# Max of three products rewritten as one part plus the relu of differences, with new PSUM pools and a new order, in an attention and feed-forward kernel

## Chip, cores, metric

One core of one Trainium2 chip. The metric is device time in microseconds (us), measured on the chip; the kernel before runs in about 255 us. A program on one core has no second die to compare with; runs over 1.5% above the fastest of their kernel count as slow and are left out of the ratios. The runs were made in jobs on several chips, and in each job the kernel before ran on the same chip in the same rounds; so kernels are compared by their ratio to it.

## The reference, cut to what matters

Batch 8, 8 heads, 576 positions, head size 64, 32 memory slots, model width 512, inner width 768.

```python
a = softmax(phi, over the 576 positions)           # (b, h, s, 32)
k_m, v_m = a^T k, a^T v                            # 32 x 64 a head
attn = softmax(q @ k_m^T / 8, over the 32 slots)
x = attn @ v_m                                     # heads side by side: (b*s, 512)
h = max(max(x @ w1, x @ w2), x @ w3)               # (b*s, 768)
out = h @ w_out                                    # (b*s, 512), float32
```

Both kernels never form x. For each batch they fold v_m into the weights (`wp` = v_m @ w, 256 x 768 for each of the three) and multiply `attn` by the folded weights.

## The kernel before

The parts that the argument touches; `...` marks cuts. P is 128, NG 2 (groups of four heads), FT 6 (768/128), S 576, SH 288, BANK 512. PSUM is where the matmuls put their results; BANK, 512 numbers a partition, is what the kernels take for one bank of it. The schedule is by hand: the order in which the instructions are written is kept.

```python
acc_pool: bufs=2, PSUM      # tiles of two banks: scores, sums, feed-forward accumulators
one_pool: bufs=4, PSUM      # tiles of one bank: transposes, k/v sums, folds, output tiles

def fold(b, ft):                                   # six a batch
    for g in range(NG):
        wps = one_pool.tile([P, 3, P], FP32)
        for i in range(2):                         # block-diagonal v: 128 rows, 64 columns
            matmul(wps[64*i : 64*(i+1)], lhsT=vm[:, 2*g+i], rhs=w_sb[:, 2*g+i, :, ft*P:(ft+1)*P])
        (scalar if g == 0 else vector).copy(out=wp[:, g, ft], in_=wps)

def ffn1(b, ft, w):                                # 6 x 3 = 18 groups a batch
    acc = acc_pool.tile([P, 2, BANK], FP32)
    ...                                            # four matmuls of 288 columns
    if w == 0:   nc.scalar.copy(out=h1, in_=a)
    elif w == 1: nc.vector.tensor_tensor(out=h2, in0=a, in1=h1, op=max)
    else:        nc.vector.tensor_tensor(out=hT[:, ft, ...], in0=a, in1=h2, op=max)

def ffn2(b, t):                                    # four or five output tiles a batch
    ...                                            # six matmuls of 512 columns, ScalarE copies, store
# order: attention(0), fold/ffn1(0), ffn2(0), attention(1) in one piece, folds(1); then for each
# batch its 18 ffn1 groups, with the next batch's attention and folds and the last batch's output
# tiles put between them at fixed fractions of the 18
```

The softmax here doesn't subtract the row's maximum and nothing guards it: scores larger than these inputs give would overflow.

## Time and profile before

| | before |
|---|---|
| median of the first 3 runs | 255.34 us (255.06 to 257.24) |
| span in the profiled run | 253.2 us, mean granted TensorE clock 0.96 |
| PE / VectorE / ScalarE busy | 195.2 / 139.1 / 121.5 us |
| one steady batch | 26.6 us |

PE is the matmul engine, DVE is VectorE, ACT is ScalarE; `L288 PE MATMUL acc<-attn,wp` is the work of line 288, its output tile and its inputs.

### The profile page before, as it was taken

The page shows a single profiled execution, that of the slowest core. Times are in us where ns is not written, and L with a number is a line of the kernel's source. Part 1 is how long each engine was busy: PE and PEld are TensorE (multiplying, and loading weights), DVE is VectorE, ACT ScalarE, POOL GpSimd, SP SyncE. Part 2 cuts the span into 40 slices and gives each one's busy share as a digit, 9 for nine tenths or more (in the row PEclk, how much of TensorE's full clock was granted, in tenths as well). Part 3 has the DMA queues.
Part 4 walks back from the last instruction along what each step waited for, and adds up shares of the span by engine and source line. Part 5 has one row for each costly group of instructions (what it writes and reads, how often), then busy time and mean ns, then how long its engine had stood idle before and what let it go on. Part 6 is the DMA issues. An engine that isn't in the chain of part 4 may idle for free.

```text
span 253.2 us, 3962 instructions
## 1 busy us (share of the span) xinstructions
PE 195.2 (77%) x1589; PEld 111.0 (44%) x1608; DVE 139.1 (55%) x252; ACT 121.5 (48%) x213; POOL 29.9 (12%) x45
## 2 busy tenths in 40 slices
PE   0176878586797889889788998897988998888970
PEld 0152333262473356445554565354734573355430
DVE  7354565056546764685196639473677465764400
ACT  2315333618524763575429462856277625733340
POOL 8533200040040003100220022000000000000000
PEclk9996799978897999999999999999999999999997
DMA  5999999999469205991397639950001500720177
GB/s 134 207 203 203 253 207 254 194 231 206 70 131 207 41 0 124 205 212 41 96 155 126 133 106 174 205 134 3 1 3 40 126 3 0 166 45 0 35 159 180
DMA packets 22786, 31.71 MB, mean 125 GB/s; under 512 B 1008, under 2 KB 17136, under 8 KB 22768
## 3 DMA queue, kind: packets, MB, share of 16 engines
q0 software_dynamic: 17776, 22.02, 47.4%
q1 hardware_dynamic: 4992, 9.44, 16.5%
q8 instruction: 12, 0.20, 0.3%
q14 instruction: 6, 0.05, 0.1%
HBM read 39.32 MB, written 9.44 MB: 193 GB/s over the span
## 4 chain that ended last, share of the span: by engine, by line
PE 47%; DVE 24%; ACT 18%; issue 4%; DMA 3%; POOL 1%; DVEq 0%; POOLq 0%
PE acc L288 19%; PE po L319 14%; DVE h L301 6%; ACT e_bd L128 6%; PE kvp L139 6%; DVE hT L304 6%; PE wps L264 5%; ACT ln L246 4%; DVE qT L189 3%; ACT h L298 3%; DMA kvo<-in_v_dram 3%; ACT r L252 3%; DVE kvn L155 2%; DVE wp L275 2%; DVE kmT L167 1%
## 5 line engine op out<-in xcount | busy, mean ns | idle before, releaser
L288 PE MATMUL acc<-attn,wp 128*128 128x288 bf16 x576 | 93.4, 295 | 17.4 <-ACT ln L246 4.8
L288 PEld LDWEIGHTS <-wp 128*128 128x128 bf16 x576 | 53.4, 99 | 52.9 <-issue 27.1
L301 DVE TENSOR_TENSOR h<-acc,h 128x576 bf16<-128x576 f32 x48 | 36.2, 754 | 50.4 <-PE acc L288 36.3
L319 PE MATMUL po<-wo_sb,hT 128*128 128x512 bf16 x197 | 48.2, 379 | 1.5 <-issue 0.5
L298 ACT CAST h<-acc 128x576 bf16<-128x576 f32 x48 | 30.6, 638 | 36.1 <-PE acc L288 35.7
L304 DVE TENSOR_TENSOR hT<-acc,h 128x576 bf16<-128x576 f32 x48 | 36.3, 756 | 8.3 <-PE acc L288 5.2
L329 ACT COPY ost<-po 128x512 f32<-128x512 f32 x32 | 18.7, 585 | 40.6 <-PE po L319 40.5
L275 DVE CAST wp<-wps 128x384 bf16<-128x384 f32 x48 | 26.2, 551 | 12.3 <-PE wps L264 12.0
L139 PE MATMUL kvp<-kvo,e_bd 128*64 128x192 bf16 x288 | 16.0, 264 | 19.7 <-DMA kvo<-in_v_dram 11.6
L319 PEld LDWEIGHTS <-hT 128*128 128x128 bf16 x216 | 20.7, 98 | 21.0 <-DVE hT L304 1.1
L273 ACT CAST wp<-wps 128x384 bf16<-128x384 f32 x48 | 22.9, 479 | 11.9 <-PE wps L264 11.6
L264 PE MATMUL wps<-w_sb,vm_bd 128*64 128x384 bf16 x192 | 26.0, 352 | 2.6 <-ACT wp L273 1.9
L139 PEld LDWEIGHTS <-e_bd 128*64 128x64 bf16 x288 | 12.9, 118 | 24.4 <-issue 13.3
L224 ACT ACTIVATE e<-sc 128x320 bf16<-128x320 f32 (+1 forms) x32 | 11.2, 414 | 25.8 <-PE sc L214 25.8
L128 ACT ACTIVATE e_bd<-ph 64x1152 bf16<-64x1152 f32 x16 | 18.6, 1161 | 4.0 <-DMA ph<-in_phi_dram 3.9
L253 DVE TENSOR_TENSOR attn<-e,r 128x576 bf16<-128x576 bf16 x16 | 12.1, 754 | 11.4 <-ACT r L252 11.4
L97 POOL DMA_DIRECT2D ph<-in_phi_dram x8 | 6.2, 772 | 94.3 <-ACT e_bd L128 90.6
L264 PEld LDWEIGHTS <-vm_bd 128*64 128x64 bf16 x192 | 7.6, 110 | 15.0 <-issue 13.7
L252 ACT ACTIVATE r<-ln 128x576 f32<-128x576 f32 x16 | 10.9, 682 | 0.5
L189 DVE COPY qT<-pt 128x1024 bf16<-128x1024 bf16 x16 | 10.8, 681 | 0.3 <-PE pt L186 0.2
L214 PE MATMUL sc<-qT,kmT 64*32 64x320 bf16 (+1 forms) x128 | 5.4, 300 | 7.1 <-DVE h L301 5.6
L246 ACT ACTIVATE ln<-sm 128x576 f32<-128x576 f32 x16 | 10.4, 650 | 0.2
(33 smaller groups left out, 91.7 us busy)
## 6 DMA issues: line engine op xcount, KB each, us to landing
out_dram<-ost SPq DMA_DIRECT2D x16, 512.0 KB, 5.3
ph<-in_phi_dram POOLq DMA_DIRECT2D x8, 576.0 KB, 4.6
kvo<-in_k_dram POOLq DMA_DIRECT2D x8, 576.0 KB, 6.4
kvo<-in_v_dram POOLq DMA_DIRECT2D x8, 576.0 KB, 8.9
qq<-in_q_dram POOLq DMA_DIRECT2D x8, 576.0 KB, 9.5
w_sb<-in_moe_w_dram POOLq DMA_DIRECT2D x6, 384.0 KB, 14.7
out_dram<-ot SPq DMA_DIRECT2D x8, 128.0 KB, 2.4
wo_sb<-in_moe_w_out_dram POOLq DMA_DIRECT2D x1, 768.0 KB, 18.6
```

Of the source, the lines that this page charges most:

```text
L128: nc.scalar.activation(out=e_bd[r, :, :, a, :], in_=ph[r], func=AF.Exp)
L139: nc.tensor.matmul(kvp[HP * i : HP * (i + 1), g, :], lhsT=e_bd[:, j, c], rhs=kv[:, :, j, c, :], start=(c == 0), stop=(c == NC - 1), tile_p ...
L246: nc.scalar.activation(out=ln.rearrange("p (h n) -> p h n", h=2), in_=sm[:, :, 0:SH], func=AF.Ln,)
L264: nc.tensor.matmul(wps[HP * i : HP * (i + 1)], lhsT=s["vm"][:, 2 * g + i], rhs=w_sb[:, 2 * g + i, :, ft * P : (ft + 1) * P], start=True, s ...
L273: nc.scalar.copy(out=s["wp"][:, g, ft], in_=wps)
L275: nc.vector.tensor_copy(out=s["wp"][:, g, ft], in_=wps)
L288: nc.tensor.matmul(acc[:, h, 0:SH], lhsT=s["wp"][:, g, ft, w, :], rhs=s["attn"][:, g, h * SH : (h + 1) * SH], start=(g == 0), stop=(g == N ...
L298: nc.scalar.copy(out=s["h1"], in_=a)
L301: nc.vector.tensor_tensor(out=h2, in0=a, in1=s["h1"], op=ALU.max)
L304: nc.vector.tensor_tensor(out=hT[:, ft, (b % 2) * S : (b % 2 + 1) * S].rearrange("p (h n) -> p h n", h=2), in0=a, in1=s["h2"], op=ALU.max,)
L319: nc.tensor.matmul(po, lhsT=hT[:, fc, c0 : c0 + P], rhs=wo_sb[:, fc, :], start=(fc == 0), stop=(fc == FT - 1),)
L329: nc.scalar.copy(out=osts[b][:, t], in_=po)
```

## The change

Its intent: max(a,b,c) = c + max(relu(a-c), b-c). The differences w1-w3 and w2-w3 are made once on the chip; c @ w_out goes through `w3o` = w3 @ w_out, also made once, folded per batch and added by two more matmuls in each output tile. So 12 accumulator groups a batch remain of 18, with one VectorE max in each pair. The folds use 64x32 tiles of the TensorE array, eight at a time, in two-bank tiles. PSUM is divided anew, the order of instructions is written out step by step, w3 and w_out load ahead of w1 and w2, and a batch's output is stored in smaller pieces (256 KB instead of 512).

```diff
-    acc_pool bufs=2;  one_pool bufs=4
+    acc_pool bufs=3;  one_pool bufs=2
-    load(0); w1,w2,w3 first halves; w1,w2,w3 second halves; w_out; load(1)
+    load(0) in two parts; w3; w_out; w1,w2 first halves; w1,w2 second halves; load(1)
+    def w3_t(f2): ...    # 24 transposes of w3
+    def w3_o(j): ...     # 24 matmuls of 512 columns: w3o = w3 @ w_out
+    def w_diff(i, h):    # four, VectorE, 16 bits, 1536 elements a partition
+        tensor_tensor(w_sb[:, :, i, half[h]] -= w_sb[:, :, 2, half[h]])
+    def slot(g, a): return a ^ (g & 1)
     def fold(b, n):                                # four a batch: three for w1-w3, w2-w3, one for w3o
+        ps = acc_pool.tile([P, NG, BANK], FP32)
+        for g, i, a: sl = slot(g, a); h4 = 2*i + sl
+            matmul(ps[32*h4 : 32*(h4+1), g, :], lhsT=vm[64 rows of a, 32 columns],
+                   rhs=w_sb[64 rows of a, ...] or w3o[...], tile_position=(64*a, 32*h4))
+        (scalar if n % 2 == 0 else vector).copy(out=..., in_=ps)      # 1024 columns
     def ffn1(b, n):                                # 12 groups a batch
-        w == 0: scalar copy; w == 1: vector max; w == 2: vector max
+        w == 0: scalar relu; w == 1: vector max
     def ffn2(b, t):
+        for g in range(NG): matmul(po, lhsT=attn[:, g, ...], rhs=wp3[b][:, g, :])
     ...
-    fill lists of positions for each batch
+    order = "F0 B0 B1 N T0 F1 Q0 F2 Q1 Q2 F3 K T1 F4 S0 S1 L F5 D0 F6 M0 T2 "
+            "D1 F7 X0 M1 D2 F8 X1 T3 F9 D3 E0 F10 T4 E1 F11"
```

In the order F is a first-product group, T an output tile, E the exp of phi, B and N the k/v sums and their scaling, Q and K transposes, S scores, M softmax sums with Ln and Exp, X their product, D a fold, L a load. Attention of batch 1 is now mixed with the output tiles of batch 0.

## The prediction

> **What bounds the kernel now.** I read the page's busy shares first, then the chain that ended last, then the costliest groups, then the busy time of each engine in stretches of one batch, and last the timeline of one batch. Busy shares, chain and groups, from the page of the kernel before:
>
> ```profile
> PE 195.2 (77%) x1589; PEld 111.0 (44%) x1608; DVE 139.1 (55%) x252; ACT 121.5 (48%) x213; POOL 29.9 (12%) x45
> ...
> PE 47%; DVE 24%; ACT 18%; issue 4%; DMA 3%; POOL 1%; DVEq 0%; POOLq 0%
> ...
> L288 PE MATMUL acc<-attn,wp 128*128 128x288 bf16 x576 | 93.4, 295 | 17.4 <-ACT ln L246 4.8
> L301 DVE TENSOR_TENSOR h<-acc,h 128x576 bf16<-128x576 f32 x48 | 36.2, 754 | 50.4 <-PE acc L288 36.3
> L319 PE MATMUL po<-wo_sb,hT 128*128 128x512 bf16 x197 | 48.2, 379 | 1.5 <-issue 0.5
> L298 ACT CAST h<-acc 128x576 bf16<-128x576 f32 x48 | 30.6, 638 | 36.1 <-PE acc L288 35.7
> L304 DVE TENSOR_TENSOR hT<-acc,h 128x576 bf16<-128x576 f32 x48 | 36.3, 756 | 8.3 <-PE acc L288 5.2
> L275 DVE CAST wp<-wps 128x384 bf16<-128x384 f32 x48 | 26.2, 551 | 12.3 <-PE wps L264 12.0
> L273 ACT CAST wp<-wps 128x384 bf16<-128x384 f32 x48 | 22.9, 479 | 11.9 <-PE wps L264 11.6
> ```
>
> PE is busy 77%, but holds only 47% of the chain; VectorE and ScalarE hold 42% between them. So the chain hops PE, ScalarE, VectorE. The first feed-forward product (L288) has three accumulators per 128 columns: one is copied by ScalarE, two go through a VectorE max. Only two accumulators exist, so PE often waits for an evacuation. Two neighbouring batches, from the stretches view (PE, weight loads, DVE, ACT, POOL busy), and the same stretches for the second product's tile `po` alone (PE, ACT):
>
> ```profile
> 93.10:119.60 26.50, 23.84 (x204) 13.64 (x206) 16.33 (x30) 15.14 (x29) 2.98 (x4) 1.00 0.71 139
> 119.60:146.30 26.70, 22.40 (x195) 13.07 (x197) 16.52 (x30) 14.85 (x28) 2.97 (x4) 1.00 0.65 126
> ```
> ```profile
> 93.10:119.60 26.50, 6.65 (x27) 2.93 (x5) 1.00 0.71 139
> 119.60:146.30 26.70, 5.40 (x22) 2.34 (x4) 1.00 0.65 126
> ```
>
> One batch takes 26.6 us. The first stretch does a fifth output tile that the second does not, 1.25 us of PE, and is not longer. So PE has slack, some 3 to 4 us a batch; the accumulator hand-over is what repeats. DMA runs at 0.65 to 0.71 of its engines and has slack there.
>
> **What the Trainium skill says.** (1) "TensorE: Matmul & The Clock Gate", section "Back-to-back issue gap": N/2.4 + 2.5 ns for a warm matmul. That is 216 ns for 512 columns; the trace agrees (six `po` matmuls hold the chain for 1.29 us, 215 ns each). For 288 columns it is 122 ns, 0.49 us for a group of four; the trace shows 1.15 us for two groups together and 0.65 for a lone one. I use 0.53 to 0.56. (2) "TensorEngine Tiling (Array Packing)", "Key Properties": different tiles execute in parallel, and changing the mode drains the engine. Trace: eight 64x32 score matmuls begin at 131.86 and the next work at 132.11, so 0.25 us for eight, where one after another they would take 0.97 by the formula above. The same page's "Gotcha 1" says that different row tiles cannot access one PSUM bank at once. The scores put each row half in its own bank; the new fold writes both row halves into one bank, in other columns of the array, so no row of this trace settles it. (3) "VectorE: DVE Perf Modes", "The perf-mode tier table": `tensor_tensor` with any PSUM operand runs at 1x; its formula (N+151)/0.96 gives 757 ns for 576, and the trace has 754 to 756. For the new 16-bit SBUF subtraction it allows 2x: estimate (768+151)/0.96 = 0.96 us for 1536 elements.
>
> **The change, part by part, for one steady batch.**
>
> Identity: max(a,b,c) = c + max(relu(a-c), b-c). The c part goes through w3@w_out, so 12 accumulators remain of 18.
>
> First product: 48 matmuls of 72, six groups of four fewer at 0.56 us: PE -3.4 us. Six VectorE maxes go: -6 x 0.755 = -4.5 us. ScalarE's six copies become six relus of the same size: 0.
>
> Second product: two more 512-column matmuls for each tile, 4.5 tiles a batch on the mean: 4.5 x 2 x 0.215 = +1.9 us of PE.
>
> Fold: before, 24 matmuls in six bursts, each holding PE 0.44 to 0.5 us with its drain, 2.8 us. After, four bursts of eight 512-column matmuls. If all eight overlap, a burst is about 0.22 + 0.2 of drain, estimated from the score burst: 1.7 us; if the two row halves take turns, 0.65 us: 2.6. I take 2.0: -0.8 us. Evacuations: from 638 ns for 576 and 479 for 384, ScalarE pays 0.83 ns an element plus 160, so 1.01 us for 1024; VectorE from 551 for 384 at 1.04 ns an element gives 1.22. ScalarE 2 x 1.01 instead of 6 x 0.479: -0.9 us. VectorE 2 x 1.22 instead of 6 x 0.551: -0.9 us.
>
> Exp of phi in four pieces instead of two: 2.73 instead of 2.32 us, ScalarE +0.4. The transposed k and v: VectorE 0.84 instead of 1.0.
>
> Sums. PE by its holding times: first product 6.7, second 7.75, k/v sums 1.8, transposes 1.55, scores 0.6, sums 0.55, folds 2.0: 21.0 us, where the same count for before gives 10.1 + 5.8 + 2.8 + 4.5 = 23.2 of 26.6. VectorE falls from 16.4 to about 11.2, ScalarE from 15.0 to 14.5. With three accumulators of two banks instead of two, and one max in the hand-over instead of two in a row, most of the 3.4 us of waits should go. What stays: the new order puts some 11 us of ScalarE work (two fold copies, two Ln/Exp pairs, exp of phi, relus, `ost` copies) behind the first fold, beside 9 to 10.7 us of PE. I allow 1 us for that: **22 us a batch**, PE-bound.
>
> **Start.** In before, the last first-product group of batch 0 is done and `po` begins at 42.1; batch 1's first product begins at 63.3, after a serial attention. In after, fold 0 needs w1 and w2 less w3. The weights and wo are, together with batch 0, the same bytes in another order; the last weight transfer of before (wo, issued 11.72, 18.6 us to landing) landed at 30.3, so I expect the last piece of w1/w2 there. Subtraction, three folds: 32. ScalarE then does batch 1's exp (2.7 us, phi landing about 33) ahead of the first relu: 36. Twelve groups at 0.53: 42.5, no gain. The w3 transposes and w3@w_out (24 matmuls each, some 7 us) hide under the load. Then attention 1 is interleaved with four output tiles: 4 x 1.72 + 1.8 + 1.55 + 0.6 + 0.55 + 2.0 = 13.4 and some 2.6 of waits: batch 1's first product begins at **58.5**, 5 us earlier.
>
> **Sum.** 58.5; batch 1, which has no output tiles beside it, 18; five batches at 22 = 110; batch 7 with 12 groups (6.4) and four tiles (6.9) and 1.2 of waits = 14.5; five last tiles of eight matmuls 8.8; from the last PE work to the end, 7.8 in before (245.4 to 253.2), a little less with smaller stores: 7.4. Total span 217.2; the measured median was 2.1 above the span: **219.3, say 219 us**, 14% less.
>
> **Rivals.** A: the gain is PE's sum alone, since waits stay as long as before (3.4 us a batch): 24.4 a batch, 5 x 2.4 + 3 more: about 234. For it: the waits may be semaphore and in-order queue delays, not accumulator shortage, and the one-bank pool shrinks from four to two while it serves `po`, transposes and k/v sums. Against it: the missing 1.25 us above shows that PE work fills waits, so they are not fixed delays.
> B: ScalarE becomes the bound. Its sum of 14.5 is far below 22, but in the second half of a batch it has about 11; with no slack there a batch is 23.5: about 228.
> C: the start gets worse: everything needs all weights, and w3@w_out adds a stage. If folds start only at 36 and PE runs at a lower clock after idling (granted clock 0.59 in 20 to 25 us of before), the start is 63 and the time 224.
> D: everything packs well, eight-fold overlap and no waits: 20.5 a batch and a start at 56: about 208.
> Slower than before would need over 27 us a batch; nothing in the sums is near it.
>
> **Range and chances.** C and B with half of A make 230; D makes 209. Range 210 to 231 around 219. Faster by over 2% means under 250: 0.96; within 2%: 0.03; slower: 0.01.
>
> **What would show it.** A steady batch of 21 to 23 us with PE busy above 90% of it, and PE's share of the chain above 65%. VectorE's total near 100 us, ScalarE's near 120. Relus of 638 ns, maxes of 756, fold copies near 1.0 (ACT) and 1.2 (DVE), subtractions near 1 us. A fold burst of 0.4 us if the eight overlap, 0.65 if the bank forces turns. First product of batch 0 ending near 42, of batch 1 beginning near 58. I am wrong if waits for the two one-bank buffers (transposes behind `ost` copies) appear on PE, if the first folds wait for weights beyond 33, or if ScalarE's queue holds accumulators.

## More of the kernel before

In the lists of waits, "A <- B: x, n, m" says that A sat idle x us in n places, at most m, until B was done. The PE rows that matter for the buffers, from the list of waits of the kernel before:

```profile
PE sc L214 <- DVE h L301: 5.6, 6, 1.9
PE acc L288 <- ACT ln L246: 4.8, 6, 0.8
PE acc L288 <- ACT h L298: 3.4, 14, 0.3
```

In each, PE wants to write a new accumulator and waits until an evacuation of an earlier one, of other data, has ended: the two-bank buffers are what it lacks.

## The result

216.91 us, median of 4 runs (216.11 to 218.64), against 255.68 (4 runs) for the kernel before. The ratio is 0.8485 (95% interval 0.8418 to 0.8552). Ratios here are the mean time of one kernel's fast runs over that of the other's of the same rounds, so not quite the ratio of the medians. The predicted 219 was 1% high.

Busy shares, the chain that ended last and costly groups, from the page of the changed kernel (in a group: its count, busy us and mean ns of one, then the idle us of the engine just before and what ended most of it):

```profile
PE 175.2 (82%) x1589; PEld 101.7 (47%) x1608; DVE 103.1 (48%) x168; ACT 119.8 (56%) x201; POOL 32.0 (15%) x48
...
PE 59%; ACT 16%; DVE 12%; issue 5%; DMA 5%; POOL 2%; DVEq 0%; ACTq 0%; POOLq 0%
...
L365 PE MATMUL acc<-attn,wp 128*128 128x288 bf16 x384 | 60.1, 286 | 7.5 <-ACT h L375 5.2
L377 DVE TENSOR_TENSOR hT<-acc,h 128x576 bf16<-128x576 f32 x48 | 36.3, 756 | 45.6 <-PE acc L365 31.4
L375 ACT ACTIVATE h<-acc 128x576 bf16<-128x576 f32 x48 | 31.2, 652 | 12.8 <-PE acc L365 12.5
L350 DVE CAST wp<-wps 128x1024 bf16<-128x1024 f32 x16 | 19.5, 1221 | 20.5 <-PE wps L330 20.5
L401 PE MATMUL po<-wp,attn 128*128 128x512 bf16 x62 | 18.6, 379 | 0.1
L348 ACT CAST wp<-wps 128x1024 bf16<-128x1024 f32 x16 | 16.0, 1007 | 0.0
```

The PE rows for these buffers in its list of waits:

```profile
PE acc L365 <- ACT h L375: 5.2, 9, 1.8
PE wps L330 <- DVE wp L350: 2.8, 6, 0.5
PE wps L330 <- ACT wp L348: 1.3, 2, 0.8
```

The first product has 384 matmuls instead of 576; one of the two rows of maxes is gone; L401 is the new w3 part. PE went from 195.2 to 175.2 us busy, DVE from 139.1 to 103.1, ACT hardly moved. Two neighbouring steady batches, cut at the start of their first output tile, from the stretches view (PE, weight loads, DVE, ACT, POOL busy, granted clock, DMA share, GB/s), and then the same stretches for tile `po` alone (PE, ACT):

```profile
80.93:103.40 22.47, 21.04 (x198) 12.01 (x201) 11.26 (x20) 14.74 (x25) 2.98 (x4) 1.00 0.79 164
103.40:124.53 21.13, 19.11 (x188) 11.35 (x190) 11.26 (x20) 14.15 (x24) 2.97 (x4) 1.00 0.78 162
```
```profile
80.93:103.40 22.47, 9.14 (x40) 2.93 (x5) 1.00 0.79 164
103.40:124.53 21.13, 7.07 (x30) 2.34 (x4) 1.00 0.78 162
```

A batch is 21.8 us on the mean. PE is busy in 94% and 90% of the two. The batch with a fifth output tile is now 1.3 us longer than the other (0.9 if the batches are cut at their first product: 22.2 and 21.4); in the kernel before it was 0.2 shorter (0.1 by the other cut). So PE work has come to cost time. Mean PE idle in a batch fell from 3.5 us (the two stretches in the prediction) to 1.7, mean PE busy from 23.1 to 20.1: of the 4.8 us saved in a batch, 3.0 are less PE work and 1.8 less waiting.

The span, cut at events of the trace:

| piece | predicted | measured |
|---|---|---|
| to the first product of batch 1 | 58.5 | 59.6 |
| batch 1 | 18 | 18.9 |
| batches 2 to 6 | 110 | 109.4 |
| batch 7 with batch 6's output tiles | 14.5 | 12.8 |
| last five output tiles | 8.8 | 9.1 |
| to the end of the span | 7.4 | 4.6 |
| span | 217.2 | 214.3 |

### The profile page after: what moved, and what is told of

It is laid out like the page before. It is cut to its first block, busy times and chain, and to the rows that moved or that the text cites. A ratio compares the mean times of both kernels' runs of the same rounds, so it can differ in the third digit from the quotient of the medians.

```text
span 214.3 us, 3857 instructions
## 1 busy us (share of the span) xinstructions
PE 175.2 (82%) x1589; PEld 101.7 (47%) x1608; DVE 103.1 (48%) x168; ACT 119.8 (56%) x201; POOL 32.0 (15%) x48
## 4 chain that ended last, share of the span: by engine, by line
PE 59%; ACT 16%; DVE 12%; issue 5%; DMA 5%; POOL 2%; DVEq 0%; ACTq 0%; POOLq 0%
PE po L392 21%; PE acc L365 15%; PE po L401 6%; DMA qq<-in_q_dram 5%; ACT e_bd L171 5%; PE kvp L185 4%; ACT e L275 4%; DVE wp L350 4%; PE po L142 3%; ACT h L375 3%; DVE hT L377 3%; PE wps L330 3%; DVE qT L235 2%; DVE attn L308 1%; POOL kvo L89 1%
## 5 line engine op out<-in xcount | busy, mean ns | idle before, releaser
L365 PE MATMUL acc<-attn,wp 128*128 128x288 bf16 x384 | 60.1, 286 | 7.5 <-ACT h L375 5.2
L392 PE MATMUL po<-wo_sb,hT 128*128 128x512 bf16 x200 | 49.7, 379 | 1.2 <-issue 0.5
L365 PEld LDWEIGHTS <-wp 128*128 128x128 bf16 x384 | 34.8, 97 | 29.2 <-issue 16.4
L375 ACT ACTIVATE h<-acc 128x576 bf16<-128x576 f32 x48 | 31.2, 652 | 12.8 <-PE acc L365 12.5
L350 DVE CAST wp<-wps 128x1024 bf16<-128x1024 f32 x16 | 19.5, 1221 | 20.5 <-PE wps L330 20.5
L171 ACT ACTIVATE e_bd<-ph 64x576 bf16<-64x576 f32 x32 | 21.8, 681 | 6.9 <-DMA ph<-in_phi_dram 6.6
L185 PEld LDWEIGHTS <-e_bd 128*64 128x64 bf16 x288 | 12.8, 117 | 16.6 <-issue 13.1
L401 PE MATMUL po<-wp,attn 128*128 128x512 bf16 x62 | 18.6, 379 | 0.1
L348 ACT CAST wp<-wps 128x1024 bf16<-128x1024 f32 x16 | 16.0, 1007 | 0.0
L330 PE MATMUL wps<-w_sb,vk 64*32 64x512 bf16 x96 | 9.4, 384 | 3.0 <-DVE wp L350 2.8
L232 PE MATMUL pt<-ident,qq 128*128 128x128 bf16 x128 | 10.4, 231 | 1.3 <-DMA qq<-in_q_dram 1.1
```

The costliest lines, as they stand in the source:

```text
L171: nc.scalar.activation(out=e_bds[b % 2][r, 2 * g : 2 * g + 2, :, slot(g, a), :], in_=ph[r, 2 * g : 2 * g + 2], func=AF.Exp,)
L185: nc.tensor.matmul(kvp[HP * i : HP * (i + 1), g, :], lhsT=e_bds[b % 2][:, j, c], rhs=kv[:, :, j, c, :], start=(c == 0), stop=(c == NC - 1) ...
L330: nc.tensor.matmul(ps[M * h4 : M * (h4 + 1), g, :], lhsT=s["vm"][a][r, 2 * g + i, sl, :], rhs=(w_sb[r, 2 * g + i, 0:2, n * W : (n + 1) * W ...
L348: nc.scalar.copy(out=out_, in_=ps)
L350: nc.vector.tensor_copy(out=out_, in_=ps)
L365: nc.tensor.matmul(acc[:, h, 0:SH], lhsT=wps[b][:, g, ft // 2, w, (ft % 2) * P : (ft % 2 + 1) * P], rhs=attn[:, g, c0 : c0 + SH], start=(g ...
```

## Experiments

The question after the result: which part of the change carries the gain? The prediction said that the kernel before lacked accumulators, and that fewer groups, a third buffer and the new order remove most waits. One rival was that PE's smaller sum is all (waits as before); another that ScalarE becomes the bound.

### The third accumulator, and the order

**b1: the kernel before with the new pools.**

```diff
-  accp bufs=2, onep bufs=4
+  accp bufs=3, onep bufs=2
```

> The kernel before with only the PSUM pools of the changed one: three two-bank accumulators and two one-bank buffers instead of two and four. Theory H (the hand-over of accumulators held the kernel before, 3.4 us of waits a batch over seven batches): the third buffer alone gives some 1 to 2 us a batch, so 242 to 250 us. Rival S (the waits come from the order of the instructions and the queues, not from the number of buffers): 254 to 258. Rival O (the one-bank pool, which here also takes twelve fold tiles a batch, becomes the wait): over 258.

Measured: 258.65 us against 256.09; ratio 1.009 (1.002 to 1.017). The same. PE's rows in its list of waits:

```profile
PE wps L264 <- DVE wp L275: 6.1, 8, 1.2
PE wps L264 <- ACT wp L273: 2.6, 2, 2.0
PE pt L186 <- DVE kvn L155: 2.5, 4, 0.7
PE pt L195 <- DVE qT L189: 2.4, 6, 0.6
```

The waits for accumulators shown before are gone, but PE now waits for one-bank buffers: for folds and transposes. The wait changed place. That is rival O's mechanism, though its number (over 258) is met only just.

**b2: as b1, with the folds in the two-bank accumulators.**

```diff
-  for g: wps = one_pool.tile([P, 3, P]); ...; copy of 384 columns (ScalarE g=0, VectorE g=1)
+  wps = acc_pool.tile([P, 2, BANK]); both g into it; one copy of 768 columns (engines by turns)
```

> The kernel before with three accumulators and two one-bank buffers as in the run before, but its folds now use the two-bank accumulators too: both halves of a fold in one tile, one evacuation of 768 columns instead of two of 384. The product of three stays (18 groups). Theory H: without the fold tiles in the one-bank pool the third accumulator shows its worth: 240 to 250 us. Rival S (three accumulators are worth nothing to 18 groups, only to twelve): 254 to 260.

Measured: 262.09 us, ratio 1.025 (1.018 to 1.032). Theory H missed again. PE waits for accumulators once more, for instance 4.4 us in six places until ScalarE's Ln. With 18 groups, neither division of the eight banks gains anything by itself under the old order.

**a1 and a2: the changed kernel with two accumulators**, and two or four one-bank buffers.

```diff
-  accp bufs=3, onep bufs=2
+  accp bufs=2, onep bufs=2      # a1
+  accp bufs=2, onep bufs=4      # a2
```

> The changed kernel with two accumulators instead of three, all else the same (two PSUM banks unused). Theory H (third accumulator carries most of the removed waits): waits come back, 1.5 to 2.5 us a batch over seven batches, so 227 to 235 us. Rival S (twelve accumulators and the new order suffice, the third buffer is spare): 216 to 219.

> The changed kernel with the pools of the kernel before: two accumulators, four one-bank buffers. Theory H: like the run with two and two, within 2 us, because the one-bank pool was not the wait: 226 to 235. Rival O (two one-bank buffers hold transposes behind output copies): up to 5 us better than two and two. Rival S: 216 to 219.

Measured: a1 238.04 us, ratio 0.919 (0.909 to 0.930), where two of its four runs were slow and are not in the ratio (the fast two: 235.6 each); a2 237.02 us, ratio 0.925 (0.917 to 0.933). In the changed kernel the third accumulator is worth some 7 to 8% of the time before, a little more than theory H said; the one-bank buffers, two or four, are worth nothing. From a2, the longest waits for accumulators, and two neighbouring steady batches, cut at their first score product:

```profile
PE acc L365 <- DVE hT L377: 8.9, 17, 0.6
PE sm L289 <- DVE wp L350: 4.3, 6, 0.8
```
```profile
119.97:143.06 23.09, 19.41 (x189) 11.51 (x190) 11.35 (x19) 14.36 (x25) 2.98 (x4) 1.00 0.70 141
143.06:167.78 24.72, 21.34 (x198) 12.13 (x200) 11.35 (x19) 14.94 (x26) 0.00 (x0) 1.00 0.49 101
```

At full clock a batch takes 23.9 us, and PE idles 3.5 us of it, as much as in the kernel before and 1.8 more than in the changed kernel.

**a8: the changed kernel with the old coarse order.**

```diff
-  order = "F0 B0 B1 N T0 ..." and batch 1's attention mixed with T0 to T3
+  T0 T1 T2 T3, then attention 1 in one piece; then the old list of positions, over 12 groups
```

> The changed kernel with the coarse order of the kernel before: attention of batch 1 in one piece after the output tiles of batch 0, the steps of the next batch spread by the old positions over twelve groups, inputs loaded two batches ahead. PE's sum is the same. Theory H: the start loses some 5 us, a batch 0.5 to 1 us: 224 to 231 us. Rival S (the order carries the gain): 232 or more. If the order is worth nothing: 217.

Measured: 225.37 us, ratio 0.879 (0.872 to 0.886). In its trace batch 1's first product begins at 64.1 instead of 59.6; the k/v sums of the steady batches begin at 89.33, 111.66, 135.11 and 157.44, by turns 22.3 and 23.5 us apart, 22.9 on the mean instead of 21.8. The start is as theory H had it (4.5 us later for "some 5"), the batch loses 1.1 us, a little more than its 0.5 to 1.

**a9: the identity alone**, with old pools and old order.

```diff
   a8, and
-  accp bufs=3, onep bufs=2
+  accp bufs=2, onep bufs=4
```

> The changed kernel with the old pools (two accumulators, four one-bank buffers) and the old coarse order: the identity with its precomputed weights and folds alone. Theory Q (the three parts work together: fewer groups, third accumulator, order): more than the sum of the single losses is not possible, so between 225 (old order) and 246; if the losses of pools (20 us) and order (8.5 us) add up, 245; if one covers the other, 237 to 240. Rival: the identity carries nearly all, 226 to 230.

Measured: 259.73 us, ratio 1.015 (1.010 to 1.020). All the expectations missed, mine worst: the identity alone, whose work is that of the changed kernel (there 20 us less PE and 36 us less VectorE time than before), gains nothing. Busy shares and the longest waits for accumulators, then three stretches of about a batch (the same columns as above):

```profile
PE 195.3 (76%) x1589; PEld 107.1 (41%) x1608; DVE 103.7 (40%) x168; ACT 120.8 (47%) x201; POOL 32.0 (12%) x48
...
PE acc L365 <- ACT wp L348: 7.5, 7, 1.2
PE acc L365 <- DVE hT L377: 5.1, 11, 0.6
```
```profile
98.00:126.00 28.00, 21.99 (x192) 11.67 (x192) 11.40 (x19) 14.71 (x26) 2.99 (x4) 0.94 0.60 132
126.00:155.00 29.00, 24.74 (x194) 13.12 (x198) 11.40 (x19) 14.43 (x25) 2.98 (x4) 0.82 0.58 118
181.50:207.50 26.00, 20.93 (x194) 12.24 (x198) 11.31 (x19) 14.23 (x25) 0.00 (x0) 1.00 0.17 41
```

Two things are to be seen. At full clock (the last) a batch takes 26.0 us with PE busy only 20.9: PE idles 5.1 us, more than the 3.5 of the kernel before. The folds are in the two accumulators now and hold each for an evacuation of 1.0 to 1.2 us, and the longest of the waits above is for one (`wp`). And in the other two the granted clock fell to 0.94 and 0.82. Its timeline (start and length in us; in brackets the wait before) shows one such fall:

```profile
110.70 0.66 PE L365 MATMUL acc<-attn,wp 128*128 128x288 bf16 x4
...
114.88 1.12 PE L365 MATMUL acc<-attn,wp 128*128 128x288 bf16 x4 [1.21 <-ACT wp L348]
```

The same four matmuls take 1.12 us instead of 0.66 after a run of short waits. Over the span PE's busy time is 195.3 us where the changed kernel, with the same 1589 matmul records, has 175.2. So of the 44 us between the two spans, up to 20 are matmuls that took longer and not waits. That the short waits lower the clock is not shown: in this same trace two waits of the same length (0.75 and 1.21 us, from 168.3 and 170.6) are followed by full clock. The comparison free of the clock is between steady batches at 1.00: 26.0 us here, 26.6 before, so even there the identity alone gains 0.6 us at most. Not run, and so open: the 12 groups with the folds left in one-bank buffers, which would part the identity from the move of its folds.

**b3: the kernel before with its own arithmetic, but the new pools and the new order.**

```diff
-  accp bufs=2, onep bufs=4; fill lists
+  accp bufs=3, onep bufs=2
+  order = "F0 B0 B1 N T0 F1 F2 Q0 F3 Q1 Q2 F4 F5 K T1 F6 F7 S0 S1 L F8 D0 F9 M0 T2 D1 F10 F11 "
+          "X0 M1 D2 F12 X1 D3 T3 F13 F14 D4 E0 F15 T4 D5 E1 F16 F17"
```

> The kernel before (18 groups, six folds, its own arithmetic) with three accumulators, two one-bank buffers and the fine order of the changed kernel, its steps placed at the same shares of 18 groups. Theory Q (before was held by order and buffers together, so that either alone could show nothing): PE's sum of 23.2 us a batch plus 1.5 of waits gives 24.7 instead of 26.6, the start gains 3: 237 to 244. Rival R (with 18 groups the evacuations or the folds in the one-bank pool hold it whatever the order): 250 to 262.

Measured: 246.5 us, ratio 0.962 (0.957 to 0.967), between the two theories. Two of its steady batches:

```profile
94.73:121.72 26.99, 23.55 (x203) 14.11 (x204) 16.63 (x31) 15.34 (x30) 2.98 (x4) 1.00 0.66 128
121.72:147.56 25.84, 22.16 (x198) 13.52 (x199) 16.63 (x31) 14.86 (x29) 2.98 (x4) 1.00 0.70 133
```

A steady batch, 26.4 us on the mean, is as good as the 26.6 of before. The 4% come from the start and the end: batch 1's first product begins at 60.0 instead of 63.3, batch 1 takes 4.0 us less, and the part behind the last steady batch 2.2 less. In the kernel before the granted clock is halved three times, 3.4 us each, between 51 and 83 us, here not once; how much of the gain at the start that is was not separated. For the steady state rival R was right.

The parts together, as ratios to the kernel before:

| | old pools | new pools |
|---|---|---|
| 18 groups, old order | 1 | 1.009 |
| 18 groups, new order | not run | 0.962 |
| 12 groups (identity), old order | 1.015 | 0.879 |
| 12 groups (identity), new order | 0.925 | 0.8485 |

Under the old order the identity without the third accumulator loses 1.5%; with it, 12% are gained; and the third accumulator without the identity gains nothing. Under the new order the identity with the old pools gains 7.5%, and the new pools without the identity gain 3.8%. PE's idle time in a steady batch tells the same of the 12 groups: 5.1 us with old pools and old order (a9), 3.5 with the new order alone (a2), 2.5 with the new pools alone (a8, two batches from 97.04 to 142.82), 1.7 with both.

### What bounds the changed kernel

**a3: without the w3 part in the output tiles** (its result is wrong: relative error 0.88).

```diff
-  for g in range(NG): matmul(po, lhsT=attn[...], rhs=wp3s[b][:, g, :])   # and its half-tile form
```

> The changed kernel without the matmuls that add the w3 part to the output tiles (its result is wrong on purpose; 36 tiles lose two 512-column matmuls each, 15.5 us of PE). Theory P (PE bounds the changed kernel, 93 per cent busy in a steady batch): nearly all of it comes out, 12 to 15 us less than 217: 202 to 205. Rival B (ScalarE in the second half of a batch bounds it): 208 to 216.

Measured: 202.61 us, ratio 0.787 (0.779 to 0.795). Two of its four runs were slow and are not in the ratio (the fast two: 199.4 and 202.2). By the ratios it is some 15.7 us below the changed kernel, for 15.5 us of PE. Theory P holds, rival B falls.

**a4: the fold on four array tiles instead of eight.**

```diff
-  def slot(g, a): return a ^ (g & 1)
+  def slot(g, a): return a
```

> The changed kernel with one line changed: the heads keep their places in both head groups, so that the eight matmuls of a fold fall on four tiles of the array, each used twice, instead of on eight. If eight tiles overlap as the trace says (0.22 us from burst to burst), a burst takes 0.43 and 32 bursts cost 0.21 each: 6.9 us of PE, of which theory P expects most in the time: 221 to 224. If PE is not the bound: 216 to 218.

Measured: 219.87 us, ratio 0.862 (0.859 to 0.864), 3 us above the changed kernel. First the starts of three bursts of eight matmuls in the changed kernel's timeline (one matmul of each), then both halves of one burst here:

```profile
33.71 0.39 PE L330 MATMUL wps<-w_sb,vk 64*32 64x512 bf16 x1
33.93 0.38 PE L330 MATMUL wps<-w_sb,vk 64*32 64x512 bf16 x1
34.15 0.38 PE L330 MATMUL wps<-w_sb,vk 64*32 64x512 bf16 x1
```
```profile
121.99 0.39 PE L330 MATMUL wps<-w3o,vk 64*32 64x512 bf16 x1
122.22 0.38 PE L330 MATMUL wps<-w3o,vk 64*32 64x512 bf16 x1
```

Eight matmuls take 0.22 us, as long as one; here four do, so a burst takes twice that. The mechanism is as expected, but only some 3 of the 6.9 us of added PE time show: a batch grew by 0.5 us for 0.86 of PE. The rest fills time in which PE was idle: its idle time in a batch falls from 1.7 to 1.3 us. Which waits it fills is not shown; those for `wps` buffers fall only from 4.1 to 3.7 us over the span.

**a5: the old order of the weight loads.**

```diff
-  w3, w3; w_out; w1, w2; w1, w2
+  w1, w2, w3; w1, w2, w3; w_out
```

> The changed kernel with the weights loaded in the old order: w1, w2, w3 by halves, then wo. All the bytes must land before batch 0's last fold in either order, so the data is there at the same time; but w3@wo, some 7 us of PE with its transposes ahead, then begins at about 30 instead of 26 and is no longer hidden. Theory: the start moves by 3 to 5 us: 220 to 222. Rival (the load order is worth nothing, the bytes decide): 216 to 218.

Measured: 221.7 us, ratio 0.868 (0.865 to 0.872), 4.8 us above the changed kernel. w3 @ w_out begins at 31.7 instead of 26.4, and the first fold at 38.7 instead of 33.7. As the theory had it.

### A better version

**c1: two pairs of exp moved at the start.** In the changed kernel ScalarE does four exps ahead of batch 0's first relu; from its timeline:

```profile
36.10 2.76 ACT L171 ACTIVATE e_bd<-ph 64x576 bf16<-64x576 f32 x4
38.89 1.19 ACT L375 ACTIVATE h<-acc 128x576 bf16<-128x576 f32 x2
```

```diff
-  steps(1, "E0", "E1"); ...; for n in range(12): steps(0, f"F{n}")
+  ...; for n in range(12): steps(0, f"F{n}"); n == 5: steps(1, "E0"); n == 11: steps(1, "E1")
-  plan for batch 1 ... ; steps(2, "E0", "E1")
+  steps(2, "E0", "E1") inside the plan, behind "Q0"
```

> The changed kernel with two pairs of exp moved at the start: batch 1's into and behind batch 0's twelve groups instead of ahead of them (ScalarE held the first relu from 36.1 to 38.9), batch 2's into the middle of batch 1's attention instead of its end (PE waited for it at 62). Theory P: the start and batch 1 lose these waits, 2 to 4 us less: 213 to 215.5. Rival: the start is held by weights and w3@wo anyway: 216 to 218.

Measured: 212.12 us, ratio 0.830 (0.826 to 0.833), the result correct. In the trace the first relu begins at 35.8 instead of 38.9, batch 1's first product at 57.6 instead of 59.6, that of batch 2 at 74.3 instead of 78.4, and the last tile ends 4.1 us earlier too. Some 0.6 us of this is there at the first fold (33.1 instead of 33.7) and is not the exps'. It beats both kernels.

**c2: as c1, with output tiles 2 and 3 copied by VectorE.**

```diff
-  nc.scalar.copy(out=osts[b][:, t], in_=po)
+  (vector if t >= 2 else scalar) copy
```

> As the run before, and output tiles 2, 3 and 4's first two copied out of PSUM by VectorE (0.68 us each by estimate) instead of ScalarE, 16 copies in all, all in the half of a batch where ScalarE has most to do. Theory P (PE bounds a batch): within 1 us of the run before. Rival B (ScalarE bounds the second half): 3 to 5 us less than it.

Measured: 213.21 us, ratio 0.833 (0.829 to 0.837): no gain over c1. Taking 16 copies off ScalarE does not help, so again ScalarE is not the bound. (The expectation's words on a fifth tile do not fit the edit: only tiles 2 and 3 of each batch were moved, 16 copies.)

## Why the prediction was right, and where its reasons were not

- **The steady batch: right, its two terms less so.** 22 us predicted, 21.8 measured; PE busy 90 to 94%, over 90 on the mean as it said. Run a3 shows PE as the bound. But 22 was 21.0 of PE work and 1.0 of waits, and 20.1 and 1.7 were measured: two errors that nearly cancel, which is luck. The chain's PE share is 59%, not above 65: that sign was set too high; ScalarE and VectorE still hold 28% of the chain.
- **Costs of single instructions: right.** Fold copies 1007 and 1221 ns for 1.01 and 1.22 us; subtractions 956 ns for 0.96 us; maxes 756. (The formula for these two stands in the cited page's section on the TRN2 errata, for 32-bit operands in SBUF; it fitted here all the same.) The relu took 652 ns, 14 more than the copy of the same size. DVE total 103 for "near 100", ACT 119.8 for "near 120". The fold burst was the good case: all eight tiles overlap.
- **The start: right within 1.1 us, by two errors that partly cancel.** w3 @ w_out was not hidden: its last matmul begins at 33.4, so the first fold began at 33.7. ScalarE's two fold copies (34.3 to 36.2) then held back the exps, and these the first relu, to 38.9 instead of 36. The twelve groups were done at 44.5 instead of 42.5; the attention with the four output tiles then took 15.0 us instead of 16.0. From 27.3 to 30.3 the matmuls of w3 @ w_out begin 0.43 us apart, later 0.215, which alone is some 1.5 us.
- **The tail: 2.8 us too long.** The stores are smaller, and from the last PE work to the end it is 4.6 us instead of 7.8 before (no run tests the cause). This term alone is most of the difference between 219 and 217.
- **The waits: the reason only half right.** The prediction counted lower PE work and fewer waits as two gains that add. a9 shows that they do not: with two accumulators and the old order, less PE work becomes idle (5.1 us a batch instead of 3.5, at full clock) and the batch is nearly that of before. b1 and b2 show that a third accumulator does nothing for 18 groups under the old order, where PE then waits for transposes and folds instead. b3 shows that the new order does not help the steady batch of 18 groups either. Rival A (waits stay as they were, 24.4 us a batch, 234 us) is what was measured for the new order without the third accumulator: a2 idles 3.5 us in a batch of 23.9, and a1 and a2 take 235.6 to 237 us. So the third accumulator is what took the rival's ground away, 1.8 us a batch. What the identity buys is room in PSUM: 12 groups and four two-bank folds where there were 18 and twelve one-bank ones. That this room is the cause is argued from b1, b2 and a9; no run has 18 groups with more than these eight banks.
- **Rival B** (ScalarE) is refuted by a3 and c2. **Rival C** partly came true: the folds began at 33.7, between the 32 of the sum and the rival's 36, and a5 shows what the new load order saved of it, some 5 us. The 2 us by which the twelve groups were late are gone in c1 (done at 42.5), so most of them hang on the exps ahead of the first relu. **Rival D**'s overlap was real, and still did not reach 208, as some waits stay.
- **Where a1's loss lies:** its span is 19.5 us longer than the changed kernel's. 12.2 of it are in batches 2 to 6, nearly all at full clock, 2.4 each, within the 1.5 to 2.5 of theory H; 2.3 in batch 1; 1.5 at the end; and 3.6 ahead of batch 1, which the theory did not count. Ahead of batch 1 and in it the granted clock was halved for a while (from 37.6 to 41.0 and from 78.5 to 85.4 us); how much of the 5.9 us that is stays open.

## What to carry to other kernels

Ask of a change that removes work not only what it takes off each engine, but which buffer it frees, and spend that buffer in the same change: here, under the old order, fewer groups or a third accumulator alone gained nothing, and both gained 12%. If the trace shows that an extra tile costs no time, PE work is not the bound, and removing PE work may not pay until the waits go too: a9 is such a case. Then look at what an engine does, in the order written, ahead of the first instruction that others wait for: moving two pairs of exp was worth 2%. And compare steady batches at the same granted clock before giving a difference to waits.

## What the Trainium skill lacked or had wrong

- "TensorE: Matmul & The Clock Gate", section "Why this matters for your kernels", advises no PE-idle gaps of over some 3 us. In a9 the clock fell (four matmuls in 1.12 instead of 0.66 us) with no wait of PE longer than 1.21 us in the 15 us ahead of it. So shorter waits are no safeguard; nor are they enough, since the same waits later left the clock full. The page does tell, in its section "A second HAM failure mode: psum-queue depth-cycling", of short idles between groups of matmuls that make the clock swing, but gives no length for them.
- The same page warns in its caveats that the clock records are not fully to be trusted. They fit the matmuls: in the changed kernel those of w3 @ w_out begin 0.43 us apart up to 30.3 and 0.215 from 30.6 on, and the first clock record, of full clock, begins at 30.46. What the page lacks: ahead of the first record there is none, and the stretches view prints 1.00 there, though the matmuls ran at half the rate.
- "TensorEngine Tiling (Array Packing)", section "Gotcha 1: PSUM Pressure", says that different row tiles cannot access the same PSUM bank at once. In the new fold, 64-row tiles of both halves write one bank, in different columns of the array; bursts of eight begin 0.22 us apart and the results are correct. At least for 64x32 tiles in different column groups the sentence is too wide.
